# A linear attention and tanh FFN kernel on one core: wider v loads, PSUM banks by choice, merged matmul bursts, and a tanh over two banks

## The chip, the cores and the metric

The kernel runs on one core of one Trainium2 chip. The metric is the device time of one execution in microseconds. A core has TensorE (matmul, "PE"; its weight loads are "PEld"), VectorE ("DVE"), ScalarE ("ACT"), GpSimd ("POOL") and SyncE ("SP", here only issuing DMAs). Each runs its own instruction queue in the order in which it was written; semaphores make one wait for another. Matmul results go to PSUM, eight banks of 128 partitions x 512 f32.

## What is computed

```
# q, k, v: 4 batches x 4 heads x 1088 tokens x 32;  S1, S2: 8 x 32
phi(x):  a = x @ S1.T;  b = x @ S2.T;  outer product of a and b  -> 64 features
kv  = sum over tokens of phi(k) (x) v          # 64 x 32 per head
z   = sum over tokens of phi(k)                # 64 per head
num = phi(q) @ kv
den = phi(q) . z + 1e-6
x   = (num / den), heads side by side          # 4352 x 128
h   = x @ w_in                                 # 128 x 2048
out = (h - tanh(h)) @ w_out                    # 2048 x 128, f32 result
```

## The kernel before

**Attention, per batch.** k is laid out with 128 partitions (4 heads x 32 token groups) and 34 tokens of 32 values in each. VectorE transposes it in blocks of 32 (kT, L502), TensorE multiplies by the sketch weights (k sketch, L522, into PSUM banks 0 and 1 of the four attention banks `bk`), VectorE transposes back (abk, L513) and forms the outer products in three pieces (w, L555). TensorE sums them with v into kv (L568, bank 2, three bursts of 24 matmuls, one for each piece of w). The denominator is not made from z: "gram" (L535, bank 3) and a small matmul (L543) give a third sketch of 8 columns, which is copied into the weights of the q side (wq, L547). kv is copied out with repeats (kvd), transposed on TensorE (L585) and copied out again (kvb). Then q: transpose (qT, L509), sketch into all four banks (L605), transpose out of PSUM (abc, L610), four small VectorE operations that fold 1/den into a, outer products (qp, L648) and their transposes (qpT, L653), and the numerator matmuls (L662), again over all four banks, whose result ScalarE copies as bf16 into xT (`x`). The numerator is done in pieces of blocks of 128 tokens: blocks 0-2, 2-5 and 5-9 for batch 0, 0-5 and 5-9 for the others. f32 matmuls show in the trace as two instructions each.

**FFN.** xT has 4352 columns, cut into ten groups (`GCOLS`: 256, 384, 448, six of 512, 192). For each of 16 blocks of d_ff: an h matmul (L759) into one of three PSUM banks, a tanh with scale -1 on ScalarE (L762) to bf16, and an o matmul with w_out (L772) accumulating in the one output bank. The linear part h @ w_out is two more matmuls (L776) with the product w_in @ w_out, held as high and low bf16 halves (wch, wcl) and made once on the chip from transposed w_in (wiT) and w_out (L740). VectorE transposes the finished group out of PSUM (ot, L781), and SP stores it.

**What sets the order.** The kernel is a list of operations with keys, given to a planner (`_Prog.schedule`). It simulates the five queues with a duration for each operation (`_pe`, `_a`, `_v` and so on, ns), takes at each step the engine that can start earliest, and among the operations that can start within a short window (`WINDOW`) the one with the smallest key. What comes out is a fixed order for each engine; `sync` then adds the semaphore waits. Attention keys are -50000 and rising, FFN keys are due times from 12500 on, loads come first. Where an operation may run on two engines, the planner chooses. Before the first use of the output bank, TensorE's longer gaps are filled with matmuls on zeros (`fill`, L368), planned at 110 ns each.

**Buffers.** `_Pool` holds single buffers; a value takes the one that comes free first. The four attention banks are four fixed values that every stage of every batch writes in turn.

**Loads.** All go through SP in a written order (k, q, v, w_in, w_out of batch 0's needs first, then k, v, q of batches 1 to 3), except that the v of batch 0 goes through ScalarE's queue. v is loaded in four DMAs of 32 partitions for each batch.

Of the kernel before, what the change touches and what calls it, by code (L numbers as in the profile page):

```python
# [9 lines left out]
NC = 34  # L10
NB = 9
# [9 lines left out]
PERIOD = 8900.0  # L21
WINDOW = {"tensor": 60.0, "vector": 150.0, "scalar": 60.0, "gpsimd": 30.0, "sync": 30.0}


class _Pool:

    def __init__(self, aps, psum=False):
        self.slots = [[ap, 0.0, []] for ap in aps]
        self.psum = psum
        self.used = False  # L30

    def seed(self, i, op):
        self.slots[i][2].append(op)


class _Val:

    def __init__(self, pool=None, ap=None, psum=False):
        self.pool = pool
        self._ap = ap  # L40
        self.psum = pool.psum if pool is not None else psum
        self.phases = []
        self.slot = None
        self.left = 0

    @property
    def ap(self):
        return self._ap if self.slot is None else self.slot[0]
# [7 lines left out]
class _Prog:  # L56
    SWITCH = 95.0
# [40 lines left out]

    def schedule(self, filler=None):
# [6 lines left out]
        free = {"tensor": 1100.0, "vector": 900.0, "scalar": 900.0, "gpsimd": 900.0, "sync": 800.0}  # L106
        self.order = {e: [] for e in free}
        dma_free = {}
        pemode = None

        def start_of(o, e):
# [9 lines left out]
            for v in o.vals:  # L121
                if v.pool is not None and v.slot is None:
                    best = None
                    for s in v.pool.slots:
                        if s[1] is not None and (best is None or s[1] < best):
                            best = s[1]
                    if best is None:
                        return None
                    t = max(t, best)
# [3 lines left out]
        while n < len(self.ops):  # L133
            best = None
            for e in free:
# [9 lines left out]
                t, o = min(((t, o) for t, o in cands if t <= t0 + WINDOW[e]), key=lambda x: (x[1].key, x[0]))  # L145
# [5 lines left out]
            for v in o.vals:  # L151
                if v.pool is not None and v.slot is None:
                    s = min((s for s in v.pool.slots if s[1] is not None), key=lambda s: s[1])
                    v.slot = s
                    v.pool.used = True
                    s[1] = None
                    for d in s[2]:
                        o.deps.setdefault(d, False)
                    v.first_deps = list(s[2])
                elif v.pool is not None and v.phases[0][2] and o in v.phases[0][2]:  # L160
                    for d in v.first_deps:
                        o.deps.setdefault(d, False)
            if e == "tensor":
                if filler is not None and t - free[e] > 350.0 and not filler[2].used:
                    self.fill(filler, free[e], t)
                if pemode is not None and o.mode != pemode:
                    t += self.SWITCH
                pemode = o.mode
            o.eng, o.t0 = e, t
            occ, o.lat = o.engs[e]  # L170
            if o.dma:
                free[e] = t + occ
                st = max(t + 1400.0, dma_free.get(e, 0.0))
                dma_free[e] = st + o.dma
                o.t1 = dma_free[e] + (600.0 if o.key < -89800 else 2000.0)
# [7 lines left out]
            for v in o.vals:  # L183
                v.left -= 1
                if v.left == 0 and v.pool is not None:
                    last = v.phases[-1][2]
                    v.slot[2] = list(last)
                    v.slot[1] = max(d.t1 + (0.0 if d.dma else d.lat) for d in last)
# [6 lines left out]
    def fill(self, filler, a, b):  # L195
        t = a
        while t + 110.0 + 200.0 < b:
            o = _Op()
            o.engs = {"tensor": (110.0, 215.0)}
# [3 lines left out]
            o.eng, o.t0, o.t1, o.lat = "tensor", t, t + 110.0, 215.0  # L203
# [86 lines left out]
def bass_polysketch_attn__then__act_tanh_shrink_kernel(  # L290
# [24 lines left out]
    def pool(name, n, shape, dtype=FP32):  # L315
        return _Pool([sb(name, shape, dtype) for _ in range(n)])
# [4 lines left out]
    bank_h = _Pool([ps("psh") for _ in range(3)], True)  # L321
    bank_o = _Pool([ps("pso") for _ in range(1)], True)
    psa = ps("psa", 4)
    bk = [_Val(ap=psa[:, i * 512:(i + 1) * 512], psum=True) for i in range(4)]
    psa4 = psa.rearrange("p (g x) -> p g x", g=4)
# [8 lines left out]
    w_p = pool("w", 3, [128, 3 * 256])  # L334
    qp_p = pool("qp", 3, [128, 3 * 256])
    qpT_p = pool("qpT", 3, [128, 5 * 256])
# [8 lines left out]
    kvb_p = pool("kvb", 2, [128, 2, 128])  # L345
    th_p = pool("th", 24, [128, 512], BF16)
    ot_p = pool("ot", 3, [128, 512])
    xT = sb("xT", [128, B * S], BF16)
# [19 lines left out]
    filler = (lambda e, n: e.matmul(bank_o.slots[0][0][:, 0:256], zz.ap[:, 0:128], zz.ap[:, 128:384], start=True, stop=True), zop, bank_o)  # L368
# [15 lines left out]
    for pl, f, val in ((kT_p, lambda a: a[:, 1088:1152], 0.0),   # L384
                       (m_p, lambda a: a[:, :, 8:9], 1e-6)):
        for i, s_ in enumerate(pl.slots):
            o = pool_op(lambda e, n, a=f(s_[0]), val=val: e.memset(a, val), n=64, key=-49000)
# [4 lines left out]
    vvals = [[_Val(ap=vL[b][g * 32:(g + 1) * 32, :, :]) for g in range(4)] for b in range(B)]  # L392
    for b in range(B):
        P.add(_v(256), lambda e, n, b=b: e.memset(vL[b][96:128, :, 224:288], 0.0), w=[vvals[b][3]], key=-89000 + b)

    def load(key, o_, i_, w, nbytes, eng="sync", rate=320.0, after=()):
        return P.add({eng: (450.0, 0.0)}, lambda e, n: e.dma_start(out=o_, in_=i_), w=w, key=key, dma=nbytes / rate,  # L397
                     after=after)

    for x, Sx, e_ in ((0, S1, "sync"), (1, S2, "scalar")):  # L400
        s_load = load(-99000, sin.ap[:, x, :], Sx[None, :, :].to_broadcast([16, 8, 32]), [sin], 16384, e_)

    kvals = [[_Val(ap=kL[b][:, 0:576]), _Val(ap=kL[b][:, 576:1088])] for b in range(B)]
# [4 lines left out]
    def load_k(key, b):  # L408
        src = k[b].rearrange("h (t c) d -> (h t) (c d)", c=NC)
        if b == 0:  # L410
            load(key, kL[b][:, 0:576], src[:, 0:576], [kvals[b][0]], 128 * 576 * 4)
            load(key + 1, kL[b][:, 576:1088], src[:, 576:1088], [kvals[b][1]], 128 * 512 * 4)
        else:
            load(key, kL[b][:, :], src[:, :], kvals[b], 128 * 1088 * 4)

    def load_v(key, b, eng="sync"):
        for g in range(4):
            w_ = (9 if g < 3 else 7) * 32
            vs = v[b].rearrange("h (t c) d -> t h (c d)", c=NC)[:, :, g * 288:g * 288 + w_]
            load(key + g, vL[b][g * 32:(g + 1) * 32, :, 0:w_], vs, [vvals[b][g]], 128 * w_ * 4, eng, rate=205.0,  # L420
                 after=[s_load] if eng == "scalar" else ())
# [19 lines left out]
    load_v(next(lk), 0, "scalar")  # L441
# [6 lines left out]
    for b in range(1, B):  # L448
        load_k(next(lk), b)
        load_v(next(lk), b)  # L450
        load_q(next(lk), b, 0)
# [35 lines left out]
    seq = [0]  # L487

    def nk():
        seq[0] += 1  # L490
        return -50000.0 + seq[0]
# [8 lines left out]
    def k_transposes(b):  # L500
        for i, (lo, hi) in enumerate(((0, 576), (576, 1088))):
            P.add(_v(hi - lo), lambda e, n, lo=lo, hi=hi: e.transpose(kT[b].ap[:, lo:hi], kL[b][:, lo:hi]),  # L502
                  r=[kvals[b][i]], w=[kT[b]], key=nk(), name=f"kT{b}.{i}")
# [7 lines left out]
    def back(b, bank, dst, n_, nm):  # L511
# [362 lines left out]
```

## Time and profile before

| | |
|---|---|
| time, median of 3 runs | 123.5 us (122.54 to 125.51) |
| span of the profiled execution, first to last instruction | 122.6 us (the page gives no other time for it) |
| instructions | 3742 |
| tanh, L762 | 160 instructions, 72.9 us busy |
| h matmuls, L759 | 52.8 us busy |
| o matmuls, L772 | 49.0 us busy |
| numerator matmuls, L662 | 10.1 us busy |
| kv matmuls, L568 | 6.9 us busy |
| first tanh, last ot (start) | 21.88 us, 119.18 us |
| ot of the ten groups (start) | 31.39, 45.47, 52.76, 67.45, 78.54, 89.39, 99.78, 108.04, 115.68, 119.18 us |
| k sketches of the four batches (start) | 8.16, 36.44, 56.79, 76.94 us |

Time lines give start and length in us, then the engine, the line of the kernel, the operation, the output and input tiles, the shape and the number of instructions merged in the line; in brackets stands how long the engine sat idle before it, and what ended that. The length of a matmul is from its start to its modelled end; matmuls overlap, so the distance between starts tells the rate. Lines of stretches give, after the interval and its length, the busy time of PE, PEld, DVE, ACT and POOL with instruction counts, then TensorE's granted clock, the busy share of the DMA engines and GB/s.

### The profile page before, as it was taken

To read this page: it belongs to the slowest core of one execution; us is meant where nothing else is said; L and a number is where in the kernel's file an instruction comes from. 1 tells how busy PE (TensorE), PEld (TensorE's weight loads), DVE (VectorE), ACT (ScalarE), POOL (GpSimd) and SP (SyncE) were. 2 spreads that over 40 slices of the span, in tenths; PEclk is the share of its full clock that TensorE was granted. 3 is DMA by queue.
4 is the path that set the end of the run, shared out by engine and by line. 5 is a ranking of instruction groups with operands and counts; after the bars stand their busy time and mean duration, and the time that the engine had idled before them with its cause. 6 is when DMAs were issued, how large, how long until landed. Compare 5 with 4: busy or idle time off the path is not lost.

```text
span 122.6 us, 3742 instructions
## 1 busy us (share of the span) xinstructions
PE 107.0 (87%) x1616; PEld 52.6 (43%) x1629; DVE 68.7 (56%) x110; ACT 85.9 (70%) x197; POOL 4.8 (4%) x24
## 2 busy tenths in 40 slices
PE   6995696849859999969999999989999999989980
PEld 4763584426424634424443444354334423233350
DVE  5529480895738999984908992662999020020210
ACT  0402661746737789777788898838988998989970
POOL 4300412000000000000000000000000000000000
PEclk9999679985999999999999999999999999999999
DMA  1999999999991004022000310050005005004052
GB/s 18 265 276 328 341 301 196 285 199 276 204 217 41 5 0 64 0 39 46 0 5 0 61 24 5 0 89 2 5 7 79 5 0 86 0 13 72 3 90 36
DMA packets 24913, 11.29 MB, mean 92 GB/s; under 512 B 19008, under 2 KB 23232, under 8 KB 24896
## 3 DMA queue, kind: packets, MB, share of 16 engines
q1 hardware_dynamic: 23760, 10.43, 38.1%
q10 hardware_dynamic: 1136, 0.62, 2.0%
q8 instruction: 13, 0.21, 0.7%
q14 instruction: 4, 0.03, 0.1%
HBM read 8.81 MB, written 2.23 MB: 90 GB/s over the span
## 4 chain that ended last, share of the span: by engine, by line
PE 57%; DVE 12%; SPq 8%; DMA 8%; issue 6%; ACT 5%; DVEq 0%
PE pso L772 22%; PE psh L759 19%; SPq L397 8%; DMA kL<-in_k_dram 8%; PE psa L662 7%; ACT th L762 5%; DVE w L555 4%; PE psa L568 3%; DVE ot L781 3%; PE pso L776 2%; DVE abc L610 2%; PE psa L605 2%; DVE abk L513 2%; PE psa L522 2%; DVE kT L502 1%
## 5 line engine op out<-in xcount | busy, mean ns | idle before, releaser
L762 ACT ACTIVATE th<-psh 128x512 bf16<-128x512 f32 (+4 forms) x160 | 72.9, 561 | 13.1 <-PE psh L759 11.5
L759 PE MATMUL psh<-xT,wi 128*128 128x512 bf16 (+4 forms) x153 | 52.8, 355 | 2.7 <-ACT xT L319 0.7
L772 PE MATMUL pso<-th,wo 128*128 128x512 bf16 (+4 forms) x154 | 49.0, 354 | 3.0 <-issue 2.2
L759 PEld LDWEIGHTS psh<-xT,wi 128*128 128x128 bf16 x160 | 15.4, 98 | 28.1 <-ACT th L762 16.9
L772 PEld LDWEIGHTS pso<-th,wo 128*128 128x128 bf16 x160 | 15.3, 100 | 14.7 <-issue 3.1
L781 DVE STREAM_TRANSPOSE ot<-pso 128x512 f32<-128x512 f32 (+4 forms) x10 | 6.2, 621 | 24.7 <-PE pso L772 24.7
L653 DVE STREAM_TRANSPOSE qpT<-qp 128x512 f32<-128x512 f32 (+1 forms) x16 | 12.4, 773 | 0.5
L648 DVE TENSOR_TENSOR qp<-ap,abc 128x512 f32<-128x512 f32 (+1 forms) x16 | 11.7, 730 | 0.2
L662 PE MATMUL psa<-qpT,kvb 32*32 32x128 f32 (+3 forms) x576 | 10.1, 285 | 1.4 <-issue 1.3
L555 DVE TENSOR_TENSOR w<-abk 128x768 f32<-128x768 f32 x12 | 10.7, 949 | 0.1
L368 PE MATMUL pso<-zz 128*128 128x256 bf16 x57 | 9.8, 337 | 1.1 <-DVE zz L367 1.1
L610 DVE STREAM_TRANSPOSE abc<-psa 128x1152 f32<-128x1152 f32 (+2 forms) x5 | 5.7, 1134 | 8.7 <-PE psa L605 8.7
L319 ACT CAST xT<-psa 128x384 bf16<-128x384 f32 (+3 forms) x13 | 5.3, 439 | 6.9 <-PE psa L662 6.9
L662 PEld LDWEIGHTS psa<-qpT,kvb 32*32 32x32 f32 x576 | 6.5, 105 | 5.5 <-issue 2.5
L502 DVE STREAM_TRANSPOSE kT<-kL 128x576 f32<-128x576 f32 (+1 forms) x8 | 5.6, 722 | 4.9 <-DMA kL<-in_k_dram 4.9
L513 DVE STREAM_TRANSPOSE abk<-psa 128x288 f32<-128x288 f32 x8 | 3.4, 462 | 8.4 <-PE psa L522 8.4
L368 PEld LDWEIGHTS pso<-zz 128*128 128x128 bf16 x57 | 6.5, 121 | 3.4 <-DVE zz L367 1.1
L568 PE MATMUL psa<-w,vL 128*32 128x64 f32 x288 | 6.9, 244 | 0.4 <-DVE w L555 0.3
L568 PEld LDWEIGHTS psa<-w,vL 128*32 128x32 f32 x288 | 5.3, 125 | 2.5 <-DVE w L555 2.0
L509 DVE STREAM_TRANSPOSE qT<-qL 128x1088 f32<-128x1088 f32 (+2 forms) x5 | 5.3, 1051 | 1.4 <-DMA qL<-in_q_dram 1.4
L319 ACT CAST wi<-wi_f 128x512 bf16<-128x512 f32 x3 | 1.9, 618 | 5.1 <-DMA wi_f<-in_moe_w_in_dram 5.1
L605 PE MATMUL psa<-qT,wq 32*32 32x288 f32 (+2 forms) x160 | 3.5, 381 | 1.5 <-ACT wq L547 1.5
(51 smaller groups left out, 50.0 us busy)
## 6 DMA issues: line engine op xcount, KB each, us to landing
kL<-in_k_dram SPq DMA_DIRECT2D x3, 544.0 KB, 12.4
qL<-in_q_dram SPq DMA_DIRECT2D x3, 544.0 KB, 14.0
vL<-in_v_dram SPq DMA_DIRECT2D x9, 144.0 KB, 12.8
wi_f<-in_moe_w_in_dram SPq DMA_DIRECT2D x4, 256.0 KB, 8.5
wo_f<-in_moe_w_out_dram SPq DMA_DIRECT2D x4, 256.0 KB, 8.8
out_dram<-ot SPq DMA_DIRECT2D x16, 64.0 KB, 2.0
out_dram<-ot SPq DMA_DIRECT2D x8, 56.0 KB, 1.9
vL<-in_v_dram ACTq DMA_DIRECT2D x3, 144.0 KB, 6.8
```

Source lines behind the costliest of these rows:

```text
L368: filler = (lambda e, n: e.matmul(bank_o.slots[0][0][:, 0:256], zz.ap[:, 0:128], zz.ap[:, 128:384], start=True, stop=True), zop, bank_o)
L397: return P.add({eng: (450.0, 0.0)}, lambda e, n: e.dma_start(out=o_, in_=i_), w=w, key=key, dma=nbytes / rate, after=after)
L555: P.add(_v(768), lambda e, n: e.tensor_tensor(out=wv.ap.rearrange("p (x i j) -> p x i j", i=8, j=8), in0=abh(0)[:, :, :, None].to_broadcas ...
L568: i = e.matmul(bk[2].ap[h * 32:(h + 1) * 32, 0:64], vL[b][:, h, blk * 32:(blk + 1) * 32], wvs[b, p].ap[:, (bi * 4 + h) * 64:(bi * 4 + h + ...
L610: P.add(_vp(sn * 4), lambda e, n: e.transpose(abc.ap.rearrange("p k h f -> p h k f")[:, :, 0:s1 - s0, :], psa4[:, :, 0:sn].rearrange("p h ...
L648: P.add(_v(cn * 256), lambda e, n, qp=qp, c0=c0, cn=cn: e.tensor_tensor(out=qp.ap[:, 0:cn * 256].rearrange("p (x i j) -> p x i j", i=8, j= ...
L653: P.add(_v(cn * 256), lambda e, n, qp=qp, o0=o0, cn=cn: e.transpose(qt.ap[:, o0 * 256:(o0 + cn) * 256], qp.ap[:, 0:cn * 256]), r=[qp], w=[ ...
L662: i = e.matmul(psa4[h * 32:(h + 1) * 32, g, 0:nb * 32], kvb.ap[g * 32:(g + 1) * 32, x, h * 32:(h + 1) * 32], qq[g * 32:(g + 1) * 32, 0:nb, ...
L759: P.add(_pe(n_ / 2.4 + 2.6), lambda e, n, jb=jb, hv=hv: e.matmul(hv.ap[:, 0:n_], wi[jb // 4].ap[:, (jb % 4) * 128:(jb % 4 + 1) * 128], xt, ...
L762: P.add(_a(n_), lambda e, n, hv=hv, th=th: e.activation(out=th.ap[:, 0:n_], in_=hv.ap[:, 0:n_], func=AF.Tanh, scale=-1.0), r=[hv], w=[th], ...
L772: fn = lambda e, n, x=x, st=st, sp_=sp_: e.matmul(ov.ap[:, 0:n_], wo[x // 4].ap[:, x % 4, :], ths[x].ap[:, 0:n_], start=st, stop=sp_)
L781: P.add(_vp(n_), lambda e, n: e.transpose(ot.ap[:, 0:n_], ov.ap[:, 0:n_]), r=[ov], w=[ot], key=-60000, name=f"ot{gi}")
```

## The change

- **v and k layout.** v is loaded in two DMAs of 64 partitions a batch, each partition with 9 or 8 consecutive tokens, all through SP. So that k's features meet the right tokens, the k transposes write their columns with a stride of two and the k sketch reads them in blocks of 32. For batches 1 to 3, q is loaded ahead of v. The two S loads go through ScalarE's queue.
- **Load cap.** Each load waits for the load that lies 1.4 MB before it to land. The planner's DMA model has one shared wire in place of one for each queue.
- **PSUM.** The eight banks are one tensor. A pool lists choices of one, two or four banks; values of a group take a choice together. Banks 0 to 2 are for h and 3 for o as before; the attention stages take one (gram, kv), two (k sketch) or four (q sketch, numerator) of banks 4 to 7. In batch 0, gram and kv use banks 2 and 1.
- **Bursts.** For batches 1 to 3 the small matmul and all of kv are one operation on TensorE; the k sketch is two operations in batch 0. The numerator is in pieces 0-2, 2-5, 5-9 (batch 0), 0-5, 5-9 (batch 1) and one piece 0-9 (batches 2 and 3). Its copy is split by halves of the four banks, and these copies, kvd and kvb may go to VectorE.
- **Late tanh.** From group 7 on, h goes to pairs of banks (4-5, 6-7, 0-1) and one tanh covers both; the output has two banks; each h also waits for the last two attention operations. 20 tanh buffers in place of 24.
- **Planner.** The keys of batch 0's first chain are lowered by 15000, and operations below -60500 may be taken up to 450 ns ahead of others. Fillers count 214 ns, in gaps over 200 ns, until the first o. Estimates of bursts are new, and a switch of tile mode counts 125 ns, not 95. A value that takes a buffer whose last user is the operation just before it on its engine waits for its end.

```diff
+FILL = (214.0, 60.0)
+CAP = 1.4e6
+PAIRS = 7
+URGENT = (-60500.0, 450.0)
+PIECES = {0: [(0, 2), (2, 5), (5, 9)], 1: [(0, 5), (5, 9)], 2: [(0, 9)], 3: [(0, 9)]}
...
-                t, o = min(((t, o) for t, o in cands if t <= t0 + WINDOW[e]), key=lambda x: (x[1].key, x[0]))
+                t, o = min(((t, o) for t, o in cands if t <= t0 + (URGENT[1] if o.key < URGENT[0] and not o.dma else WINDOW[e])), key=lambda x: (x[1].key, x[0]))
...
-                if filler is not None and t - free[e] > 350.0 and not filler[2].used:
+                if o.name == "o0.0":
+                    fills = False
+                if filler is not None and t - free[e] > 200.0 and fills:
                     self.fill(filler, free[e], t)
...
-                st = max(t + 1400.0, dma_free.get(e, 0.0))
-                dma_free[e] = st + o.dma
-                o.t1 = dma_free[e] + (600.0 if o.key < -89800 else 2000.0)
+                wire = max(t + 1450.0, wire) + o.dma
+                o.t1 = wire + (300.0 if o.key < -79000 else 2000.0)
...
-    bank_h = _Pool([ps("psh") for _ in range(3)], True)
-    bank_o = _Pool([ps("pso") for _ in range(1)], True)
-    psa = ps("psa", 4)
-    bk = [_Val(ap=psa[:, i * 512:(i + 1) * 512], psum=True) for i in range(4)]
+    psall = ps("psb", 8)
+    pb = [_Bank() for _ in range(8)]
+    bank = lambda i, n=1: psall[:, i * 512:(i + n) * 512]
+    one = lambda *x: _Pool([([pb[i]], [bank(i)]) for i in x], True)
+    bank_h = one(0, 1, 2)
+    bank_o = one(3)
+    bank_o2 = one(3, 2)
+    pair_h = _Pool([(pb[i:i + 2], [bank(i, 2)]) for i in (4, 6, 0)], True)
+    att1 = one(4, 5, 6, 7)
+    att2 = _Pool([(pb[i:i + 2], [bank(i), bank(i + 1)]) for i in (4, 6)], True)
+    att4 = _Pool([(pb[4:8], [bank(4, 2), bank(6, 2)])], True)
...
+    def load(key, o_, i_, w, nbytes, eng="sync", rate=330.0, cap=True):
+        after = []
+        if cap:
+            left = CAP - nbytes
+            for op, nb in reversed(loads):
+                left -= nb
+                if left < 0:
+                    after = [op]
+                    break
...
+    def load_v(key, b):
+        vs = v[b].rearrange("h (m x) d -> m h (x d)", x=17)
+        for e in range(2):
+            w_ = 256 if e else 288
+            load(key + e, vL[b][e * 64:(e + 1) * 64, :, 0:w_], vs[:, :, e * 288:e * 288 + w_], [vvals[b][e]], 64 * w_ * 16)
...
+            P.add(_v(nb * 64), lambda e, n, e_=e_, nb=nb: e.transpose(
+                kT[b].ap.rearrange("p (j u t r) -> p r j u t", u=2, t=32, r=2)[:, :, 0:nb, e_, :],
+                kL[b].rearrange("p (r j t) -> p r j t", r=2, t=32)[:, :, e_ * 9:e_ * 9 + nb, :]),
+                r=[kvals[b][e_]], w=[kT[b]], key=nk(), name=f"kT{b}.{e_}")
...
+        def mm(e, n):
+            scmm(b, e)
+            for p in range(3):
+                i = kv_part(b, p, e)
+            return i
+        P.add(_pe(1070), mm, r=[wvs[b, p] for p in range(3)] + vvals[b] + [s2r, gms[b]], w=[pv[b]], key=nk(),
+              mode="128x32", name=f"sckv{b}")
...
-        P.add(_pe(max(nb * 32 / 1.2, 110) * 4 + 60), num, r=[kvb, qt], w=bk, key=nk(), mode="32x32", name=f"num{b}.{b0}")
+        P.add(_pe(max(nb * 32 / 1.2, 215.0) * 4), num, r=[kvb, qt], w=pn, key=nk(), mode="32x32", name=f"num{b}.{b0}")
+        for hf in range(2):
+            kn = min(nb, (NC - b0 * 4 - hf * 2 + 3) // 4)
+            xv = _Val(ap=xT[:, col0 + hf * 64:col0 + hf * 64 + kn * 128].rearrange("p (k y) -> p k y", y=128)[:, :, 0:64])
+            P.add({**_a(kn * 64), **_vp(kn * 64)}, lambda e, n, hf=hf, kn=kn, xv=xv: copy(
...
+        late = gi >= PAIRS
+        ov = _Val(bank_o2 if late else bank_o)
+        m = 2 if late else 1
...
+            if jb % m == 0:
+                hv, th = _Val(pair_h if late else bank_h), _Val(th2_p if late else th_p)
...
+                P.add(_a(n_ * m), lambda e, n, hv=hv, th=th: e.activation(
+                    out=th.ap.rearrange("p (u x) -> p u x", u=m)[:, :, 0:n_],
+                    in_=hv.ap.rearrange("p (u x) -> p u x", u=m)[:, :, 0:n_], func=AF.Tanh, scale=-1.0),
...
+    attention()
+    att_end = P.ops[-2:]
     weights()
```

## The prediction

> **What bounds the kernel now.** I read the page's busy and slice rows first, then the waits, then the order of time on single engines, because the shares of a whole span hide stages with different limits.
>
> ```profile
> PE 107.0 (87%) x1616; PEld 52.6 (43%) x1629; DVE 68.7 (56%) x110; ACT 85.9 (70%) x197; POOL 4.8 (4%) x24
> PEclk9999679985999999999999999999999999999999
> GB/s 18 265 276 328 341 301 196 285 199 276 204 217 41 5 0 64 0 39 46 0 5 0 61 24 5 0 89 2 5 7 79 5 0 86 0 13 72 3 90 36
> ```
>
> TensorE is the busiest engine, but its clock dips in slices 5, 6, 9 and 10, that is before 31 us: the head is loose. The loads fill slices 2 to 12 (to 37 us) at 200 to 340 GB/s. The stretches (busy time of each engine in 5 us) show the same:
>
> ```profile
> 25.00:30.00 5.00, 3.41 (x47) 2.21 (x47) 4.08 (x6) 2.92 (x9) 0.00 (x0) 0.69 1.05 230
> 70.00:75.00 5.00, 4.84 (x85) 2.11 (x84) 4.31 (x7) 4.73 (x10) 0.00 (x0) 1.00 0.19 31
> ```
>
> From 35 us on TensorE is the limit with ScalarE close behind. Where the head loses its time is seen in the order of time of the single engines:
>
> ```profile
> 1.12 7.11 PE L368 MATMUL pso<-zz 128*128 128x256 bf16 x40 [1.12 <-DVE zz L367]
> 8.16 0.72 PE L522 MATMUL psa<-kT,wab 64*32 64x288 f32 x16
> 12.68 0.62 ACT L319 CAST wi<-wi_f 128x512 bf16<-128x512 f32 x1 [1.45 <-DMA wi_f<-in_moe_w_in_dram]
> 13.21 0.16 ACT L547 COPY wq<-psa 128x8 f32<-128x8 f32 x1
> 21.80 0.78 DVE L502 STREAM_TRANSPOSE kT<-kL 128x576 f32<-128x576 f32 x1 [3.82 <-DMA kL<-in_k_dram]
> 22.50 1.07 DVE L610 STREAM_TRANSPOSE abc<-psa 128x896 f32<-128x896 f32 x1
> 31.39 0.45 DVE L781 STREAM_TRANSPOSE ot<-pso 128x256 f32<-128x256 f32 x1 [2.21 <-PE pso L772]
> 31.77 0.67 DVE L653 STREAM_TRANSPOSE qpT<-qp 128x512 f32<-128x512 f32 x1
> 35.10 0.48 PE L662 MATMUL psa<-qpT,kvb 32*32 32x128 f32 x24 [1.26 <-issue]
> ```
>
> Each pair is an engine queue written in the wrong order: 40 fillers that the planner takes for 110 ns (7.11/40 = 178 ns in the trace) hold the k sketch, whose input was ready at 4.79 + 1.43 = 6.22; a weight cast that waits for its DMA holds the small copy that the q sketch needs; k of batch 1, still on the wire, holds abc; ot, which waits for the end of column group 0, holds the last transpose of batch 0.
>
> In the middle the cost is the tile-mode switch around each attention burst, and in the tail the tanh:
>
> ```profile
> 71.46 0.38 PE L759 MATMUL psh<-xT,wi 128*128 128x512 bf16 x1
> 71.82 1.18 PE L662 MATMUL psa<-qpT,kvb 32*32 32x160 f32 x64
> 73.16 0.38 PE L759 MATMUL psh<-xT,wi 128*128 128x512 bf16 x1 [0.16 <-issue]
> 101.85 7.95 ACT L762 ACTIVATE th<-psh 128x512 bf16<-128x512 f32 x16 [0.31 <-PE psh L759]
> ```
>
> FFN matmuls of 512 columns start 0.216 us apart (a group is 34 of them, 7.34 us). A numerator of 5 blocks costs from 71.46 + 0.22 to 73.16, 1.48 us; the one of 4 blocks behind it (74.67 + 0.22 to 76.20) 1.31.
>
> **The change part by part.** The sum is made against the span of 122.6 us. The page gives the profiled execution no other time; the median of the runs is 123.5, so 0.9 is added at the end.
>
> *Head, first piece of batch 0.* Fillers are planned at 214 ns (trace 178) and only into real gaps: the k sketch can start at 6.3 instead of 8.16, 1.9 us. The abk transposes ended at 9.84 and w at 12.56; w now ends near 10.7. The wq copy is moved ahead of the casts (keys of batch 0 get -15000, and a wider window where below -60500), so the q sketch is done by then and abc starts at 10.7, not 14.12: 3.4. From abc to the end of qpT was 14.12 to 17.05, 2.9; so 13.6. The kvb copy had stood behind a 1.01 us wiT copy to 18.55; gram and kv use banks 2 and 1 in batch 0 and the copies may go to VectorE, so it is no longer last. Numerator and x copy took 18.60 to 19.86, 1.26: x at 14.9 instead of 19.86. Term: -4.9, between 0 (x waits for something else) and -5.5.
>
> *Head, rest of batch 0.* From that x to the last x of batch 0 was 19.86 to 36.32. On this chain lie wc behind a wo cast (0.9), kT in front of abc (21.62, where the sketch was done, to 22.50: 0.9), ot in front of qpT (29.18 to 31.77: 2.6), and TensorE's stop inside the numerator (1.3): 5.7. The load order by one shared wire speaks to the second, the rest only so far as the plan is better, and the stop shows no releaser. I take half, -2.8; ends 0 and -5.7.
>
> *Loads.* v goes from 16 issues of 32 partitions to 8 of 64, all on SP; an issue takes 0.43 to 0.5 us, so about 2 us of SP time go from the later batches, and 4 issues leave ScalarE's queue. The slices with 196 to 217 GB/s lie where v of later batches moves, against 301 to 341 before; nearest rows for the wide form. New waits: each load waits for one 1.4 MB earlier, and behind it on SP stand all later loads and the first stores. The first k load landed 3.3 us after its issue; 1.4 MB in 3.3 us is 424 GB/s, above what moves, so I cost the cap at nothing. Its cover is that landing time; at 6 us it would be 233 GB/s, and the 5.44 MB to the end of batch 1's v would come at 2 + 23 = 25 us. The k sketch of batch 1 is now at 36.44 and would be near 28, so even that holds. The strided kT write and moving operand have no row: same element counts, 0 to +0.7 us per batch (a transpose doubled), taken at 0 because the head of batch 1 to 3 has kT done early.
>
> *Starvation.* Batch 0 feeds 1088 x 34/512 x 0.216 = 15.6 us of FFN; batch 1's first x came 16.0 us after its k sketch (36.44 to 52.46). FFN starting at 15 with some 7 us of attention bursts in it runs dry near 38, x of batch 1 comes near 28.7 + 16 = 45 if unmended, near 41 if the b0 chain is at its best. +2 (0 to +6).
>
> *kv merged, batches 1 to 3.* In batch 3 the small matmuls and three bursts took 79.81 to 80.81, 81.03 to 81.59 and 82.04 to 82.83: 2.35 us of TensorE. One burst: 72 records at the 14 to 15 ns of a burst's inside ((0.54 - 0.19)/24) is 1.05, the 8 others 0.1, one entry and exit (0.09 + 0.16): 1.4. So -0.95 each, -2.9. It gives back: kv starts when all of w is done, not at the third, +0.7 of latency in the attention chain.
>
> *Numerator merged, batches 2 and 3.* 1.48 + 1.31 = 2.79 becomes 64 records of 288 columns; the q sketch has 32 of that width from 63.68 to 64.47, 0.79 with its switches, so 1.4 to 1.6. -1.2 each, -2.4. Given back: x of the first half waits for the last transpose, which FFN feels only if it has run dry. TensorE loses 5.3 us in all, but the attention chain on VectorE (some 17 us of the 20.4 between k sketches) is next late, and ScalarE after it. I count -3; ends 0 and -5.3.
>
> *Copies on either engine.* ScalarE waited 6.9 us for numerators (xT) and 1.7 for kv; the new burst estimate (860 ns where 593 stood, trace 1.31 to 1.48) and two halves on two engines take some of it. No own term; it is the cover for the -3.
>
> *Late tanh.* From the 16 in a row: (7.95 - 0.635)/15 = 0.488; from five of 256: (1.49 - 0.386)/4 = 0.276. So 0.83 ns a column and 0.064 fixed. 24 pairs save 24 x 0.064 = 1.5. A second output bank removes the 0.31 stop at a group's start, twice. The tail's three groups took 8.26 + 7.64 + 3.50 = 19.4; TensorE's own floor is 2.375 x 7.34 = 17.4. I take -1.5; ends 0 and -2.
>
> The Trainium skill (ScalarE: Activation LUTs, What ACT_TABLE_LOAD costs) gives 186 ns fixed with 93 ns of overlap, so 93 a piece: by it the pairs would save 2.2 instead of 1.5. The trace's 0.064 decides.
>
> Sum: 122.6 - 4.9 - 2.8 + 2 - 3 - 1.5 = 112.4, with 0.9 for the median: 113.3. All ends at their best: -18.5, 105.
>
> One row speaks against it: thinner fillers. In 10 to 20 us TensorE was 3.25 to 4.34 of 5 busy with the clock at 0.82, and after the stop at 25.1 it gave 256 columns in 0.21 us instead of 0.11, for 3 us. At half clock through the head, batch 0's bursts (0.72 + 0.53 + 2.06 + 0.85 + 0.66 = 4.8) cost up to 5 more, and the gain of the head would be 3.
>
> The Trainium skill (TensorE: Matmul & The Clock Gate, What's actually happening) says that full clock needs about 3.4 us of sustained work, which is a rule against planning each filler twice as long; by it the head's bursts could all run at half clock, by the row only part of them do.
>
> **The rivals.** *Only bursts and tail gain* (17%): the head's chains wait for something else (clock, loads, TensorE's unexplained stops). For: the stops are not in the plan, and the wire is full to 37 us. Against: four queue orders are mended that stand in the trace. 122.6 - 3 - 1.5 + 0.9 = 119; with some of the head 117.
>
> *The attention chain on VectorE sets the end* (8%, slower). The late groups' h now wait for the last two x copies; behind the first such h on TensorE stand the o matmuls planned after it, and 19 us follow. Counted back from ot, group 7's first h ran near 98.4, 1.3 us after the last x (97.11), so the wait is not the last to end now. If merging adds 0.7 (kv) and copies on VectorE add 0.74 (kvd, kvb) and 1.2 (x, 640 + 448 columns), 2.7 a batch, three batches put the end of attention from 97.1 to 105: 122.6 + 8 - 1.5 + 0.9 = 130. It decides once the three batches add more than the head gives, 6 us. Against: VectorE idles 3.4 us a batch before abc and 1.7 to 3.4 before abk, which is where these copies fall.
>
> *The gain stays on paper* (7%): the plan shifts the stalls (starvation at its end, +6), and the time is 121 to 124.
>
> **How the numbers follow.** Forecast 68%, its own range 107 to 118. The range 107 to 121 holds nearly all of it and of the first rival; left out are the slower one, most of the last, and the best ends. A measurement of this kernel tells 2% from no change, that is 121.0 and 126.0. Faster: 0.68 + 0.15 = 0.83; same 0.02 + 0.06 = 0.08; slower 0.09.
>
> **What would show it.** The k sketch of batch 0 near 6.3 us, the first x near 15, the k sketch of batch 1 near 28, the last x of attention at 86 to 91. Bursts: one kv burst of about 1.4 us from batch 1 on, one numerator of 1.5 in batches 2 and 3. Tail: pairs at about 0.92 us. Wrong if the first x stays past 18, if the clock is under 0.7 through the head, or if late groups wait for attention with ScalarE idle for more than 2 us.

## The result, and the profile after

The changed kernel takes 113.65 us (median of 4 runs, 113.15 to 114.65) beside 123.04 for the kernel before: a ratio of 0.928, 95% interval 0.920 to 0.936. Medians, here and below, are of all runs, but ratios are of the fast ones alone, without those that took over 1.5% longer than the fastest of their kernel (125.51 of the kernel before is one). The profiled execution has a span of 112.6 us, 10.0 less. First the page of the changed kernel: engines, clock and GB/s.

```profile
PE 100.3 (89%) x1467; PEld 48.7 (43%) x1477; DVE 72.1 (64%) x115; ACT 79.9 (71%) x164; POOL 5.6 (5%) x25
PEclk9999999999999999999999999999999999999999
GB/s 21 259 245 329 255 232 234 243 241 272 226 270 218 165 5 69 0 47 46 0 6 0 44 49 6 6 11 83 0 6 68 25 0 93 0 12 77 4 55 73
```

In this profile the clock no longer dips. The loads last about as long as before (to slice 14 of 2.8 us, 39 us) at a lower rate, and yet the head is faster. The stretches that were shown of before, and one more from the tail (PE, PEld, DVE, ACT, POOL, clock, DMA share, GB/s):

```profile
25.00:30.00 5.00, 4.09 (x147) 2.60 (x119) 4.93 (x10) 2.89 (x8) 0.00 (x0) 1.00 0.88 258
...
70.00:75.00 5.00, 4.36 (x50) 1.67 (x50) 3.01 (x5) 4.42 (x10) 0.00 (x0) 1.00 0.01 3
...
95.00:100.00 5.00, 5.00 (x23) 1.83 (x23) 0.72 (x1) 5.00 (x7) 0.00 (x0) 1.00 0.02 3
```

From 25 to 30 us TensorE is at full clock where it was at 0.69. In the tail TensorE and ScalarE are both full. Now the order of time on single engines, head and bursts, in the changed kernel. TensorE:

```profile
1.12 4.24 PE L435 MATMUL psb<-zz 128*128 128x256 bf16 x19 [1.12 <-DVE zz L434]
6.03 1.22 PE L599 MATMUL psb<-kT,wab 64*32 64x288 f32 x16 [0.67 <-DVE kT L583]
...
10.52 0.29 PE L845 MATMUL psb<-identb,wi 128*128 128x128 bf16 x1 [1.24 <-POOL wi L375]
...
12.17 0.53 PE L724 MATMUL psb<-qT,wq 32*32 32x64 f32 x32
...
35.03 1.19 PE L671 MATMUL psb<-w,vL 128*32 128x64 f32 x72
...
65.52 0.38 PE L896 MATMUL psb<-xT,wch 128*128 128x512 bf16 x1
65.83 1.60 PE L783 MATMUL psb<-qpT,kvb 32*32 32x288 f32 x64
67.59 0.38 PE L896 MATMUL psb<-xT,wcl 128*128 128x512 bf16 x1 [0.16 <-issue]
```

VectorE and ScalarE:

```profile
12.88 0.45 DVE L729 STREAM_TRANSPOSE abc<-psb 128x256 f32<-128x256 f32 x1 [1.61 <-PE psb L724]
...
15.04 0.42 DVE L375 COPY kvb<-psb 128x256 f32<-128x256 f32 x1 [0.54 <-PE psb L703]
```

```profile
16.87 1.92 ACT L375 COPY wiT<-psb 128x1024 bf16<-128x1024 bf16 x2
18.68 0.28 ACT L375 CAST xT<-psb 128x128 bf16<-128x128 f32 x1
```

The k sketch starts at 6.03, as forecast. But the q sketch comes only at 12.17: TensorE had stopped at 9.3 for a transpose of w_in whose cast was not done. The first x is complete at 18.96, not 14.9, its second half behind two wiT copies. The merged numerator takes from 65.52 + 0.22 to 67.59, 1.85 us, a little above the forecast's 1.4 to 1.6, and the merged kv burst 1.19 from start to end, a little under its 1.4.

One division of the span is used in all that follows: up to the last x of batch 0, and behind it.

| | before | changed | changed, second profile |
|---|---|---|---|
| first x complete | 19.86 | 18.96 | 18.21 |
| last x of batch 0 | 36.32 | 29.32 | 28.58 |
| last x of attention | 97.11 | 84.37 | 83.65 |
| span | 122.6 | 112.6 | 111.9 |
| span behind the last x of batch 0 | 86.3 | 83.3 | 83.3 |

In the first profiles the head gave 7.0 us and all the rest 3.0.

### The profile page after: what moved, and what is told of

It is laid out like the page before. It is cut to its first block, busy times and chain, and to the rows that moved or that the text cites. A ratio compares the mean times of both kernels' runs of the same rounds, so it can differ in the third digit from the quotient of the medians.

```text
span 112.6 us, 3409 instructions
## 1 busy us (share of the span) xinstructions
PE 100.3 (89%) x1467; PEld 48.7 (43%) x1477; DVE 72.1 (64%) x115; ACT 79.9 (71%) x164; POOL 5.6 (5%) x25
## 4 chain that ended last, share of the span: by engine, by line
PE 36%; ACT 28%; DVE 16%; DMA 13%; issue 2%; SPq 1%; DVEq 0%
ACT th L881 25%; PE psb L892 11%; PE psb L877 10%; DMA qL<-in_q_dram 5%; DMA wo_f<-in_moe_w_out_dram 5%; PE psb L783 5%; DVE qp L767 4%; DVE qpT L772 4%; DVE abc L729 3%; DMA kL<-in_k_dram 3%; PE psb L724 3%; PE psb L671 3%; DVE ot L901 2%; PE psb L610 2%; ACT wiT L375 2%
## 5 line engine op out<-in xcount | busy, mean ns | idle before, releaser
L881 ACT ACTIVATE th<-psb 128x512 bf16<-128x512 f32 (+4 forms) x136 | 69.5, 624 | 7.4 <-PE psb L877 6.6
L877 PE MATMUL psb<-xT,wi 128*128 128x512 bf16 (+4 forms) x155 | 50.1, 349 | 1.5 <-DVE xT L375 0.5
L892 PE MATMUL psb<-th,wo 128*128 128x512 bf16 (+4 forms) x157 | 48.2, 348 | 1.4 <-DVE ot L901 0.6
L877 PEld LDWEIGHTS psb<-xT,wi 128*128 128x128 bf16 x160 | 14.9, 97 | 25.3 <-ACT th L881 14.4
L892 PEld LDWEIGHTS psb<-th,wo 128*128 128x128 bf16 x160 | 14.6, 97 | 15.7 <-ACT th L881 7.5
L901 DVE STREAM_TRANSPOSE ot<-psb 128x512 f32<-128x512 f32 (+4 forms) x10 | 6.3, 626 | 22.6 <-PE psb L892 22.6
L772 DVE STREAM_TRANSPOSE qpT<-qp 128x768 f32<-128x768 f32 (+1 forms) x14 | 12.1, 861 | 0.4
L767 DVE TENSOR_TENSOR qp<-ap,abc 128x768 f32<-128x768 f32 (+1 forms) x14 | 11.5, 818 | 0.1
L435 PE MATMUL psb<-zz 128*128 128x256 bf16 x33 | 7.8, 388 | 1.1 <-DVE zz L434 1.1
L783 PE MATMUL psb<-qpT,kvb 32*32 32x128 f32 (+4 forms) x448 | 8.3, 309 | 0.1
```

What stands on the lines that cost most here:

```text
L435: filler = (lambda e, n: e.matmul(bank(3)[:, 0:256], zz.ap[:, 0:128], zz.ap[:, 128:384], start=True, stop=True), zop)
L767: P.add(_v(cn * 256), lambda e, n, qp=qp, c0=c0, cn=cn: e.tensor_tensor(out=qp.ap[:, 0:cn * 256].rearrange("p (x i j) -> p x i j", i=8, j= ...
L772: P.add(_v(cn * 256), lambda e, n, qp=qp, o0=o0, cn=cn: e.transpose(qt.ap[:, o0 * 256:(o0 + cn) * 256], qp.ap[:, 0:cn * 256]), r=[qp], w=[ ...
L783: i = e.matmul(psa4[h * 32:(h + 1) * 32, g, 0:nb * 32], kvb.ap[g * 32:(g + 1) * 32, x, h * 32:(h + 1) * 32], qq[g * 32:(g + 1) * 32, 0:nb, ...
L877: P.add(_pe(n_ / 2.4 + 2.6), lambda e, n, jb=jb, hv=hv: e.matmul(hv.ap[:, jb % m * 512:jb % m * 512 + n_], wi[jb // 4].ap[:, (jb % 4) * 12 ...
L881: P.add(_a(n_ * m), lambda e, n, hv=hv, th=th: e.activation(out=th.ap.rearrange("p (u x) -> p u x", u=m)[:, :, 0:n_], in_=hv.ap.rearrange( ...
```

## The experiments

Twelve kernels ran, in three sets of four; those of a set ran on one chip. The kernel before took 124.72, 123.15 and 124.22 us in the three sets, so ratios are compared, and stages are read from one profile each.

| run | median us | ratio, 95% interval | last x of batch 0 | last x | span | span behind batch 0 |
|---|---|---|---|---|---|---|
| k_serial | 116.36 | 0.933 (0.924 to 0.942) | 29.3 | 91.9 | 114.8 | 85.5 |
| unmerged | 122.14 | 0.979 (0.970 to 0.988) | 28.8 | 81.3 | 119.2 | 90.4 |
| single_tanh | 115.39 | 0.926 (0.918 to 0.934) | 28.4 | 83.1 | 112.8 | 84.4 |
| old_v | 113.85 | 0.912 (0.901 to 0.922) | 28.3 | 83.0 | 111.9 | 83.6 |
| after_control | 114.09 | 0.932 (0.927 to 0.937) | 28.6 | 83.7 | 111.9 | 83.3 |
| serial_unmerged | 115.77 | 0.944 (0.937 to 0.951) | 28.9 | 89.0 | 113.1 | 84.2 |
| wit_late | 114.03 | 0.926 by the medians, no interval | 28.0 | 82.7 | 111.3 | 83.3 |
| cap_off | 121.07 | 0.979 (0.971 to 0.988) | 30.5 | 89.6 | 117.8 | 87.3 |
| before_cap | 119.32 | 0.965 (0.948 to 0.982) | 30.6 | 91.5 | 116.7 | 86.1 |
| old_fill | 115.26 | 0.936 (0.927 to 0.944) | 29.2 | 84.0 | 112.8 | 83.6 |
| no_urgent | 112.14 | 0.907 (0.897 to 0.918) | 27.3 | 82.6 | 110.3 | 83.0 |
| wit_late_old_v | 114.81 | 0.923 (0.911 to 0.936) | 27.3 | 82.7 | 112.1 | 84.8 |

**First set: the middle and the tail.** My first theory was that the free choice of banks had made the gain: the k sketch of batch 2 starts at 36.15 in the changed kernel, ahead of batch 1's q sketch, and the distance of the abc transposes fell from 20.5 us to 16.5. So this order was forbidden (k_serial).

```diff
-            P.add(_pe(485), sk2, r=[kT[b], wab], w=pk, key=nk(), mode="64x32", name=f"ksk{b}")
+            P.add(_pe(485), sk2, r=[kT[b], wab], w=pk, key=nk(), mode="64x32", name=f"ksk{b}",
+                  after=xlast[b - 1])
```

> The changed kernel, but the k sketch of each later batch waits for the last two numerator copies of the batch before, as it did when all stages shared the four banks. Theory (the free choice of banks lets the k side of the next batch run among the q steps of this one, and that is what shortened the attention period from 20.4 to 16.5 us): the period goes back to 19 to 20.5 us, the last x comes near 93 instead of 84.3, and the time is 118 to 121 us. Rival (the merged bursts shortened the period): the period stays under 17.5 and the time at 113.5 to 115.

The period went back (abc at 39.05, 59.33, 79.95) and the last x to 91.9, as the theory said. But the span grew by only 2.2 us, the ratio stays inside the changed kernel's interval, and the 116.36 us lie between the two expectations. So the theory held for the period and fell for the time: of the 7.5 us by which attention ends later, most is made good by an FFN that has less left. I then took the sum of the FFN's and attention's work for what bounds the stretch; serial_unmerged below speaks against that too.

The second kernel took the merging back.

```diff
-PIECES = {0: [(0, 2), (2, 5), (5, 9)], 1: [(0, 5), (5, 9)], 2: [(0, 9)], 3: [(0, 9)]}
+PIECES = {0: [(0, 2), (2, 5), (5, 9)], 1: [(0, 5), (5, 9)], 2: [(0, 5), (5, 9)], 3: [(0, 5), (5, 9)]}
...
     def kv_mm(b):
-        if b == 0:
+        if True:
```

> The changed kernel with kv again in three bursts and the small matmul apart in every batch, and two numerators in batches 2 and 3. Theory of the banks: TensorE gets some 5 us more work, but it is not the last to end once attention is done, so 114.5 to 116.5 us. Rival (the merged bursts carry the middle): 118 to 120 us, with the last x past 89.

The ratio went to 0.979. The 122.14 us lie beyond even the rival's 118 to 120, and yet the last x comes at 81.3 and not past 89. The order of time on TensorE tells of another cause:

```profile
45.74 1.28 PE L892 MATMUL psb<-th,wo 128*128 128x448 bf16 x5
49.20 0.54 PE L671 MATMUL psb<-w,vL 128*32 128x64 f32 x24 [2.17 <-DVE w L659]
50.06 0.54 PE L671 MATMUL psb<-w,vL 128*32 128x64 f32 x24 [0.33 <-DVE w L659]
51.10 0.44 PE L703 MATMUL psb<-ident,kvd 128*128 128x128 f32 x2 [0.49 <-ACT kvd L375]
51.47 0.86 PE L610 MATMUL psb<-kT,wab 64*32 64x288 f32 x16
53.29 1.74 PE L783 MATMUL psb<-qpT,kvb 32*32 32x160 f32 x64 [0.96 <-DVE abk L616]
```

The planner had moved batch 2's kv bursts ahead of batch 1's numerator, which needs all four banks. The FFN had run out of columns and TensorE waited for w; the numerator came at 53.29 instead of 45.72 in the control. This is the price of a plan, not of the bursts; for that the order has to be held fixed, which serial_unmerged in the second set does.

The third kernel set `PAIRS = 10`, so that no group is late.

> The changed kernel with one bank for each tanh and one output bank to the end, and no wait of the late groups for attention. As ScalarE has no pause from 84 us on, the theory that it bounds the tail gives 24 times 0.064 us for the pairs and two stops of 0.3: 115 to 116.5 us. Rival (late groups are held by the wait for attention, and the pairs only make that good): 112.5 to 114 us.

By the ratio nothing was lost (0.926 against 0.932). In the trace the stretch behind batch 0 grew by 1.1 us, and the last three groups' ot went back from 17.5 us to 19.4. The late groups' edits together give about 1 us at most; the time alone doesn't show it. The pairs themselves save little: in the changed kernel 16 pairs of 512 columns start 0.94 us apart (90.29 to 105.28), where single ones before them start 0.48 apart. More comes from the starts of the groups: in single_tanh the starts of two neighbouring tanhs are 1.11 us apart at one and 1.07 at the next, instead of 0.48, and in the changed kernel no two pairs start more than 1.04 us apart.

The fourth had v in four loads of 32 partitions and k's plain layout.

```diff
-        vs = v[b].rearrange("h (m x) d -> m h (x d)", x=17)
-        for e in range(2):
+        for g in range(4):
+            w_ = (9 if g < 3 else 7) * 32
+            vs = v[b].rearrange("h (t c) d -> t h (c d)", c=NC)[:, :, g * 288:g * 288 + w_]
```

> The changed kernel with k and v laid out as before: v in four loads of 32 partitions a batch, k in one piece for each partition, plain k transposes and k sketch. Theory (the wide v load is worth little; what it changes is SP time and the order of landing): 113 to 115 us, with the loads done 0 to 3 us later than 38 us. Rival (the narrow loads held the wire back, and the head gained from the wide ones): 116 us or more, and the last x of batch 0 past 31.

The span is the control's, 111.9, and the ratio 0.912 is not worse. The wide loads are worth nothing that shows here (the control ran in another set).

**Second set: bursts, weights, the limit on loads.** The changed kernel itself ran as a control.

> The changed kernel itself, beside the three others, so that they are compared with it on one chip. 113 to 115.5 us, ratio to the kernel before 0.92 to 0.94.

It gave 0.932. Serial_unmerged has the edits of k_serial and unmerged together.

> Both taken back at once: the k sketch of a later batch waits for the numerators before it, and kv and the numerators are in their old bursts. With the order of the batches held fixed, what is left is the price of the bursts. Theory (from the first x to the end the sum of TensorE and ScalarE work is the limit, not the attention chain: forcing the k sketch moved the last x by 7.5 us and the end by 2.2): 5 us more TensorE work come out nearly in full, 118.5 to 121 us, with the last x at 93 to 97. Rival (the bursts cost little, and the 122 us of the run without merging came from one starvation of the FFN near 50 us alone): 116 to 118 us.

1.2 us of span and 1.2% more than the control: the rival, and with 115.77 less than its 116 us. The theory that the sum of the work is the limit fell: merging and the choice of banks together are worth some 1.2 us, though the bursts alone take some 5 us from TensorE. The share of each isn't settled: with the k sketch held back, the merged kernel (k_serial) has the longer span, 114.8 to 113.1, and the lower ratio, 0.933 to 0.944, in different sets.

Wit_late took the transposes of w_in out of the way of the first x.

```diff
-                    r=[wi[jb // 4], identb], w=[tp], key=T_FIRST + 1000 + 4000 * i, mode="128x128", name=f"wit{jb}")
+                    r=[wi[jb // 4], identb], w=[tp], key=T_FIRST + 1000 + 4000 * i, mode="128x128", name=f"wit{jb}",
+                    after=xfirst)
```

> The changed kernel, but the 16 transposes of w_in wait for the first x copies of batch 0, so that neither TensorE (idle 1.24 us at 9.3 for a cast) nor ScalarE (1.92 us of copies before the second half of the first x) holds that chain. Theory (these two stand in front of the first x): it ends near 16 instead of 18.96 us, and the first tanh comes at 17.5 instead of 20.0. If total work is the limit the time falls by 1 to 2.5 us against the changed kernel; rival (the FFN then runs dry before batch 1's x at 48, or the wire is late): within 0.7 us of it.

The first x came a little earlier, in halves at 16.7 and 17.8 (control 18.2), the last of batch 0 by 0.6 and the span by 0.6; the medians are the same, 114.03 and 114.09, but with runs from 112.76 to 116.77 a gain of 1 us is not excluded. So the transposes were a cause of the late first x, not all of it. That the end does not follow the first x is told by no_urgent below.

Cap_off is the run that moved the study: `CAP = 1e9`, with which the planner wrote the same order of instructions on every engine. Nothing but SP's waits differs.

> The changed kernel without the limit of 1.4 MB on loads in flight. Theory (the limit costs wire time, 0.88 of the DMA engines busy and 250 GB/s from 15 to 35 us where 1.05 and 260 stood before, but the loads needed next come sooner): loads are done 1 to 3 us earlier, k of batch 1 comes later, and the time is 0 to 2 us longer. Rival (the limit holds the weights back, whose casts wait 7.5 us in all): 1 to 2 us shorter, with the first x before 18.

5.9 us of span more than the control, and a ratio of 0.979 beside 0.932. The loads were done earlier, as the theory said, but the loss is not k coming late. Of the 5.9 us, 1.9 stand at the last x of batch 0 and 4.0 behind it. TensorE's order of time in cap_off:

```profile
26.23 0.79 PE L783 MATMUL psb<-qpT,kvb 32*32 32x96 f32 x44 [1.30 <-issue]
...
30.26 0.27 PE L892 MATMUL psb<-th,wo 128*128 128x256 bf16 x1
33.82 1.22 PE L610 MATMUL psb<-kT,wab 64*32 64x288 f32 x16 [3.29 <-issue]
```

TensorE stops in the midst of a numerator, where no instruction waits for another engine, and for 3.29 us ahead of a k sketch whose input was ready. "Issue" means that the profile shows no cause. The waits of TensorE from 20 to 37 us, first before, then cap_off:

```profile
PE pso L772 <- issue: 1.6, 1, 1.6
PE psa L662 <- issue: 1.3, 1, 1.3
```

```profile
PE psb L610 <- issue: 3.3, 1, 3.3
PE psb L783 <- issue: 1.3, 1, 1.3
```

The kernel before has two such stops, 1.59 and 1.26 us, cap_off those of 1.30 and 3.29 and one of 0.24. In none of the twelve profiles with the limit is one longer than 0.33. What goes with them is a backlog. In cap_off v's loads of 256 KB land 12.2 us after their issue (median), in the control 4.9.

**Third set: the limit alone, and the planner's edits.** Before_cap is the kernel before with the limit added after planning, so that its order is untouched.

```diff
-    P.schedule(filler)
+    P.schedule(filler); _cap(loads)
...
+def _cap(loads):
+    for i, (op, nb) in enumerate(loads):
+        left = 1.4e6 - nb
+        for d, n_ in reversed(loads[:i]):
+            left -= n_
+            if left < 0:
+                op.deps[d] = False
+                break
```

> The kernel before, its order of instructions untouched on every engine, with one thing of the change added: each load waits for the load 1.4 MB before it to land. Theory (a deep backlog of loads stops TensorE at 25.1 and 33.8 us, where the profile names no releaser, and drops its clock behind it; the limit removes both): these two stops are gone, the last x of batch 0 comes 3 to 5 us earlier than 36.3 and the time is 118 to 121 us. Rival (the stops belong to the order of the new plan, and the limit only pays there): the stops stay and the time is within 1.5 us of the kernel before.

Both stops are gone, and the last x of batch 0 comes at 30.63 instead of 36.32. The first stop and the broken numerator of the kernel before, and the same numerator in before_cap:

```profile
26.72 0.28 PE L772 MATMUL pso<-th,wo 128*128 128x256 bf16 x1 [1.59 <-issue]
...
32.97 0.87 PE L662 MATMUL psa<-qpT,kvb 32*32 32x128 f32 x40
```

```profile
28.93 1.07 PE L662 MATMUL psa<-qpT,kvb 32*32 32x128 f32 x64
```

The ratio is 0.965 (0.948 to 0.982): about half of what the whole change gives, from waits on one queue that computes nothing. Not all of the 5.7 us in the head are the stops. k of batch 1 also lands earlier, and the second abc, which stands behind its transpose, starts at 20.99 instead of 22.50:

```profile
20.29 0.78 DVE L502 STREAM_TRANSPOSE kT<-kL 128x576 f32<-128x576 f32 x1 [3.91 <-DMA kL<-in_k_dram]
```

The other 4.2 us come behind that abc, where the stops and the slow clock were. The clock row and the same stretch of before_cap, where TensorE had been 3.41 busy at a clock of 0.69 without the limit:

```profile
PEclk9998599999999999999999999999999999999999
```

```profile
25.00:30.00 5.00, 4.43 (x143) 2.40 (x143) 4.96 (x8) 3.27 (x9) 0.00 (x0) 1.00 0.79 241
```

Old_fill brings the fillers back to 110 ns each; all other instructions keep their order.

> The changed kernel with fillers planned at 110 ns again; the order of all other instructions is the same. Theory (36 fillers in place of 19 ahead of the first k sketch hold it by 17 times 0.178 us, 3.0, and part of that is left at the end): k sketch near 8 to 9 us, time 1 to 3 us longer than the changed kernel. Rival (more fillers keep TensorE's clock up in 10 to 20 us, where runs of one order showed 0.72 to 1.00, and the later stages wait for loads anyway): within 0.7 us.

The k sketch came at 6.69, not at 8 to 9: the 36 fillers took 157 ns each and held it by 0.65 us beside the control's 6.04. The ratio is 0.936 against 0.932, with 0.9 us of span more than the control and 0.2 more than the first profile: between the two expectations and inside the intervals.

No_urgent takes the priority of batch 0's first chain back.

```diff
-        bias[0] = -15000.0
+        bias[0] = 0.0
...
-                t, o = min(((t, o) for t, o in cands if t <= t0 + (URGENT[1] if o.key < URGENT[0] and not o.dma else WINDOW[e])), key=lambda x: (x[1].key, x[0]))
+                t, o = min(((t, o) for t, o in cands if t <= t0 + WINDOW[e]), key=lambda x: (x[1].key, x[0]))
```

> The changed kernel with the keys of batch 0's first chain and the window of the others as before. Theory (the order of the head's queues, not their durations, moved the first x from 19.86 to 18.2): the first x ends at 19 to 21 us and the time is 0.5 to 3 us longer than the changed kernel. Rival (TensorE's and ScalarE's waits for weights decide there, as the transposes of w_in did): within 0.7 us.

Both were wrong on the time. The first x is later, 20.4, as the theory had it, and yet the kernel is faster: 0.907 (0.897 to 0.918), below the changed kernel's intervals in the two other sets, with the lowest median of the study. VectorE's order of time in no_urgent:

```profile
10.77 1.04 DVE L592 STREAM_TRANSPOSE qT<-qL 128x832 f32<-128x832 f32 x1
13.37 0.45 DVE L729 STREAM_TRANSPOSE abc<-psb 128x256 f32<-128x256 f32 x1 [1.56 <-PE psb L724]
...
17.93 1.07 DVE L729 STREAM_TRANSPOSE abc<-psb 128x896 f32<-128x896 f32 x1
```

The large q transpose now falls in VectorE's pause before abc; with the priority it was put off to 16.74, behind the first chain, and the second abc came at 19.94 (control 19.19). The last x of batch 0 is at 27.31, where the control has 28.58. The edit moves other operations too, so that this transpose makes the gain is read from the trace and not shown alone.

The last run put wit_late and old_v together.

> Both small gains put together: v and k laid out as before and the transposes of w_in behind the first x. If each is worth what its spans showed (0.6 and 0 us), 112.5 to 114 us, the fastest of the study; if they are noise, the changed kernel's 0.93 of the kernel before.

It gave 0.923, no better than its parts. Its last x of batch 0 is the earliest, 27.28, but a stop without a releaser in the k sketch behind it takes this back:

```profile
27.30 0.69 PE L608 MATMUL psb<-kT,wab 64*32 64x288 f32 x11
28.21 0.68 PE L608 MATMUL psb<-kT,wab 64*32 64x288 f32 x5 [0.21 <-issue]
```

From there to the last ot (107.59 us in both) it runs as wit_late does.

## Why the prediction was right, and where not

The forecast was 113.3 us and 0.83 for faster; measured were 113.65. The sum held, 112.4 us of span beside 112.6. Its terms did not, so each is set against its measurement. (The 0.9 added for the median is not what lies between a span and its time: in the runs that list both it is about 2 us. By that, both profiled executions were about 1 us above their medians, and the difference still came out.)

- *First x, -4.9.* Measured -0.9 and -1.7. The filler step held (k sketch at 6.03). The step that failed is "the q sketch is done by then and abc starts at 10.7": abc started at 12.88, because the new order has its own wrong turn, a w_in transpose on TensorE ahead of the sketch. That was not all: in wit_late, without it, the sketch still stands behind two kv bursts, and abc starts at 12.32. And the term was aimed at the wrong event: no_urgent has a later first x than before and the best time.
- *Rest of batch 0, -2.8.* Measured 16.5 to 10.4, -6.1. The mis-sized part is that "the stop shows no releaser" and I took half of a sum that held only one of the two stops (1.3 us, not the 1.59 at 25.1). By before_cap, in the old order, 4.2 us of this stretch go with the stops and the slow clock behind the first of them.
- *Loads: "I cost the cap at nothing".* This is the step that failed outright. The limit alone, in the old order, took 5.7 us off the head and 5.9 off the span (3.5% by the ratio); without it the changed kernel's span is 5.9 longer. I had priced only what it could cost, the landing of later loads, and not what a shorter backlog relieves. The row was in view: TensorE's only long stops without a releaser lay where the DMA engines were full.
- *v in wide loads, no term.* Right: old_v shows no loss.
- *Middle, +2 for starvation and -3 for bursts, and tail, -1.5.* Together -2.5; behind the last x of batch 0 the span fell by 3.0. Starvation does not show: TensorE is busy for 8.99 of the 10 us from 40 to 50 in the control. The bursts had about the lengths that I gave them, but together with the banks they are worth about 1.2, not 3: most of the 5 us is matched by more FFN work left at the end (28.2 us from the last x of attention to the end of the span in the control, 24.2 in serial_unmerged). The tail is about 1 (84.4 to 83.3 in the stretch behind batch 0), and less of it from the pairs than the 24 x 0.064 us of the sum.
- *The choice of banks* had no term. It moved the last x by 7.5 us and the end by 2.2 at most, for the reason just given.
- *The rivals.* Late groups did not hold the end: ScalarE runs almost without a pause from 84.43 us on. The attention period became shorter, 16.5 us for 20.5, not longer. And the row that spoke against the change, thinner fillers, did not decide: the clock is 1.00 from 10 to 20 us in one profile of the changed kernel and 0.83 in the other.

So the number was right in part by luck: an overestimate of queue order in the first chain stood against an underestimate of the limit on loads.

## What to carry to other kernels

Look for stops of TensorE with no releaser while loads are queued deep, and try a limit on the bytes in flight before any reordering: it needs one wait for each load, and here it gave half of the gain by itself. Look for the event that the end follows. In six profiles of the changed plan (changed, control, wit_late, old_v, old_fill, no_urgent) the span is the last x of batch 0 plus 83.0 to 83.6 us, while the kernel with the latest first x of them is the fastest. This holds only while nothing stops TensorE behind that x: it is 84.8 in wit_late_old_v, half of the difference from its stop in the next k sketch and half from a later end of the last store, and 87.3 in cap_off. An engine relieved by 5 us need not give the end that much (here some 1.2); measure merges with the order held fixed, since a planner's new order can cost more than the merge (unmerged, 5%).

## What the runs showed of the hardware

TensorE's long stops end at nearly the same distance from another event in the trace: the end of a packet of 16 KB on the instruction queue. Before, two of them end at 25.17 and 33.62 us and the stops at 26.72 and 35.10; in cap_off they end at 24.77 and 32.45 and the stops at 26.23 and 33.82. That is 1.37 to 1.55 us each time.

A count of TensorE's records (matmuls, weight loads and semaphore instructions, in order of their start) says more. In both kernels 705 records stand before the first of these stops and 961 before the second, though the two kernels do different work there. 256 records lie between, which is 64 bytes for each in 16 KB. The short stops fall into the same steps: the 0.24 us in cap_off behind 449 records, at 17.73 us, 1.39 after a packet's end, and the 0.21 in wit_late_old_v behind 961, at 28.21, 1.43 after one. In the changed kernel the packets of cap_off's two long stops end 4.7 and 4.1 us earlier, at 20.05 and 28.40, and the records that follow (24.88 and 30.09) find them there. In all 14 traces, with the packets of 16 KB and the steps of 256 taken in order, no record at a step starts less than 1.19 us after the end of its packet.

So TensorE waits at these stops, as I read them, for its own code, which comes late behind the loads. No run changed the fetching of code alone: the limit's worth is shown by experiment, and this cause only by the agreement of the traces. The Trainium skill (Runtime: NRT & Kernel Launch, Instruction fetch mechanics) says that instructions are streamed in 16 KiB blocks over a DMA queue and that the cost of crossing a block is mostly hidden; if the stops are this, it was not hidden here behind a full backlog.

Behind the two longest stops the granted clock fell: to 0.50 from 28 to 30 us in the kernel before (stop of 1.59 us) and to 0.50 from 34 to 36 in cap_off (3.29). Behind those of 1.30 and 1.26 it stayed at 1.00.

The clock in the head varies between profiles of one kernel: 1.00 and 0.83 from 10 to 20 us in the changed kernel, and 0.83 with the 36 fillers of old_fill. More fillers did not raise it in that profile.
